# T5-bias attention followed by a mixture of adapters: PV by head, logits merged into the adapter product, gates on GpSimd, x transposed by DMA

## The chip, the cores and the metric

One NeuronCore of a Trainium2 chip runs the kernel. The time is that of the whole launch on the device, in microseconds. The engines are TensorE (PE in the profile, with its weight loads as PEld), VectorE (DVE), ScalarE (ACT), GpSimd (POOL) and SyncE (SP), which only issues transfers. Each engine takes its own instructions strictly in order and waits on semaphores for the others.

## The reference

Two stages. Shapes: B = 8 batches, H = 8 heads, S = 576 positions, D = 64; the mixture sees N = 4608 rows of 512, with E = 8 experts of rank r = 16.

```
scores = q @ k.T / sqrt(D) + bias_table[bucket(|i-j|)]      # per batch and head
attn   = softmax(scores);   x = attn @ v                    # x: 4608 x 512
logits = x @ w_gate                                         # 4608 x 8
top two of the 8 experts; w = softmax over those two logits
out    = x + sum over the two experts e of w_e * (x @ A[e]) @ B[e]
```

## The kernel before, in words

**Units of work.** A *pair* is two heads of one batch; there are 32 pairs, four to a batch. Of the 576 positions 512 form four main tiles of 128, and the last 64, the *tail*, are handled for two heads at a time, so that they fill 128 partitions.

**One pair.** SyncE loads k, v and q in fp32 (`nat_dma`, `q_dma`; two 128 KB transfers each for k and v, one of 256 KB for q). GpSimd casts them to bf16 (`ck_`, `cq_`, `cv_`, all through `bcopy`, L140). TensorE transposes k and q (`T_pe`, L249) and VectorE copies the result out of PSUM (`T_ev`, L255). Five score chunks follow (`qk`, L266 for the four main ones). ScalarE takes the exponential of each 128x1024 chunk (`softmax_exp`, L286). VectorE multiplies the band near the diagonal by a table of bias factors (`band`, L295); both of its inputs are in SBUF. Then `pv` multiplies by v in six parts, for both heads inside each part (L310, L317, L325), into one PSUM tile of two banks. `norm1` takes the reciprocal of the row sums (L330) and `norm2` writes the normalised x in bf16 (L338), both for the two heads together. The first part of the next pair's `pv` waits for `norm2`, since there is one such PSUM tile.

**One mixture**, once for each of the first seven batches, after its fourth pair: TensorE transposes x (`mx_pe`, L349, and `mxt_pe`, L361, for the tail) and VectorE copies the results (`mx_ev`, L355, `mxt_ev`, L366). `lp_pe` (L379) computes the logits as products 8 columns wide. `gate_chain` (L388 to L436) turns them into gates: nine small steps, all but the exponential on VectorE. `z_pe` (L443) multiplies x by A, 128 columns wide. `z_ev` (L452) multiplies that by the gates while it reads PSUM. `zT_pe` and `zT_ev` transpose once more, `o_pe` (L468) multiplies by B, `o_ev` (L473) adds x, and `o_st` (L477) stores two tiles of 512 KB through SyncE. The tails of two batches are done together, in odd batches. The last batch has its own code (`final`), which the change leaves nearly as it is.

**Tails of k, q and v** are loaded by SyncE once per batch (`tail_dma`, `vtail_dma`: six transfers of 64 KB).

**What sets the order.** The text of the kernel does not run in the order in which it is written. Each step is entered with `add(engine, cost, function, deps, due)`; a planner at the end (L984 to L1013) walks all engines in modelled time, picks for each the ready step with the earliest due time, and so writes out a fixed order for every engine. The costs and due times are constants in the code. Buffer counts also shape it: five load buffers (`loads`), three for cast k and q (`nat`), two PSUM banks for everything small (`misc_ps`, the ring `ms`), two score tiles, two banks for `pv`, three x tiles, three output tiles.

Of the kernel before, what the change touches and what calls it, by code (L numbers as in the profile page):

```python
# [27 lines left out]
def kernel(  # L28
# [28 lines left out]
    DVE, PL, AC, SY, PE = nc.vector, nc.gpsimd, nc.scalar, nc.sync, nc.tensor  # L57
# [14 lines left out]
    class Op:  # L72
        __slots__ = ("eng", "cost", "lat", "fn", "deps", "due", "ring", "end", "done",
                     "users", "left", "ready", "n", "dma", "ps")

    QA = 0
    WARM = 40
    LAT = {"PE": 190, "ACT": 190, "DVE": 110, "PL": 200, "SP": 5000}
# [3 lines left out]
    def add(eng, cost, fn, deps=(), due=0.0, lat=None, ring=None, nb=0.0, dma=None, ps=False):  # L82
        o = Op()
        o.ps = ps
        o.dma = dma
        o.eng, o.cost, o.fn, o.due, o.ring = eng, cost, fn, due, ring
        o.lat = LAT[eng] if lat is None else lat
        o.deps = [d for d in deps if d is not None]
        o.end, o.users, o.done, o.ready, o.n = None, [], False, nb, len(ops)
        ops.append(o)  # L90
        return o
# [37 lines left out]
    Ab = cp.tile([128, 4, ER], BF16, tag="Ab")  # L129
    Wb = cp.tile([128, 4, E], BF16, tag="Wb")  # L130
# [12 lines left out]
    CC = {"PL": 650, "DVE": 330, "ACT": 520}  # L143
# [20 lines left out]
    def vtail_dma(b, e):  # L164
        if e == 0:
            stg[(b, "vtf")] = ldp.tile([128, HP, D], FP32, name="vtf", tag="vtf", bufs=2)
        SY.dma_start(out=stg[(b, "vtf")][e * 64:(e + 1) * 64],
                     in_=v[b, :, S4:, :].rearrange("(c e) p d -> e p c d", e=2)[e])

    def load(i):  # L170
        t0 = 5.0 * i
        nk = (0, 3000, 8500, 11000, 13000)[i] if i < 5 else 6500 + 1030 * (t0 - 12)
        nv = (4000, 9500, 12000, 15000)[i] if i < 4 else 6500 + 1030 * (t0 - 8)
# [9 lines left out]
    def loadt(b, due):  # L183
        n = 0.0 if b == 0 else 14000.0 if b == 1 else 6500 + 1030 * due
        for w in range(2):
            for e in range(2):
                en = "SP"
                R["lt", b, w, e] = add(en, 550, lambda w=w, e=e, en=en: tail_dma(b, w, e, en), [g_("ct", b - 2)],
                                       due + .01 * e, nb=n, dma=290)
        for e in range(2):  # L190
            R["lvt", b, e] = add("SP", 550, lambda e=e: vtail_dma(b, e), [g_("cvt", b - 2)],
# [106 lines left out]
    def pv(i, part):  # L298
        b, hp = divmod(i, HP)
        vn, vt = vnb[i], vts[b % 2]  # L300
        if part == 0:
            a = acp.tile([128, 2, S4], FP32, name="pv", tag="pv")
            st[(i, "acc")] = a[:, :, 0:5 * D1].rearrange("p h (s d) -> p h s d", s=5)
        acc = st[(i, "acc")]
        if part < 4:
            p = probs.pop((i, part))
            for h in range(2):
                for s in range(4):
                    o = h * 512 + s * 128
                    PE.matmul(acc[:, h, s, :], lhsT=p[:, o:o + 128], rhs=vn[:, part, h, :],  # L310
                              start=(part == 0 and s == 0), stop=False,
                              skip_group_check=True)
        elif part == 4:
            p = probs[(i, 4)]
            for g in range(4):
                for h in range(2):
                    PE.matmul(acc[:, h, 4, :], lhsT=p[:, g * 128:(g + 1) * 128],  # L317
                              rhs=vn[:, g, h, :], start=False, stop=False,
                              skip_group_check=True)
        else:  # L320
            p = probs.pop((i, 4))
            for s in range(5):
                l = p[:, 512 + s * 128:640 + s * 128] if s < 4 else ptt[b][:, hp, :]
                for h in range(2):
                    PE.matmul(acc[:, h, s, :], lhsT=l, rhs=vt[:, hp, h * D1:(h + 1) * D1],  # L325
                              start=False, stop=True, skip_group_check=True)

    def norm1(i):
        rc = sp.tile([128, 2, 5], FP32, name="rc", tag="rc")
        DVE.reciprocal(rc, st[(i, "acc")][:, :, :, D])  # L330
        st[(i, "rc")] = rc

    def norm2(i, s0=0, s1=5):
        b, hp = divmod(i, HP)
        acc, rc = st[(i, "acc")], st[(i, "rc")]
        if hp == 0:
            xs[b] = xp.tile([128, 5, H, D], BF16, name="x", tag="x", bufs=3)
        DVE.tensor_tensor(  # L338
            xs[b][:, s0:s1, 2 * hp:2 * hp + 2, :].rearrange("p s h d -> p h s d"),
            acc[:, :, s0:s1, :D],  # L340
            rc[:, :, s0:s1].unsqueeze(3).to_broadcast((128, 2, s1 - s0, D)), op=ALU.mult)


    def mx_pe(b, half, t2):
        if t2 == 0:
            st[(b, "xps", half)] = msp.tile([128, 4, 256], BF16, name="xps", tag="ms")
        ps = st[(b, "xps", half)]
        for c in range(4):
            PE.transpose(ps[:, c, t2 * 128:(t2 + 1) * 128],  # L349
                         xs[b][:, 2 * half + t2, 2 * c:2 * c + 2, :], ident)  # L350

    def mx_ev(b, half):
        if half == 0:
            st[(b, "m")] = xp.tile([128, 4, S4], BF16, name="xT", tag="xT")
        DVE.tensor_copy(st[(b, "m")][:, :, half * 256:(half + 1) * 256],  # L355
                        st.pop((b, "xps", half)))

    def mxt_pe(b):
        st[(b, "xtps")] = ps = msp.tile([128, 4, 2, 64], BF16, name="xtps", tag="ms")
        for c in range(4):  # L360
            PE.transpose(ps[:, c].rearrange("p f q -> p (f q)"),  # L361
                         xs[b][:, 4, 2 * c:2 * c + 2, :], ident)

    def mxt_ev(b, hf):
        s = slice(hf * 64, (hf + 1) * 64)
        DVE.tensor_copy(xts[(b // 2) % 2][s, :, b % 2, :], st[(b, "xtps")][s, :, hf, :])  # L366
# [5 lines left out]

    def lp_pe(b, w, nt, t0, t1):
        if t0 == 0:
            st[(b, w, "lp")] = msp.tile([128, nt, E], FP32, name="lp", tag="ms")
        lp, xT = st[(b, w, "lp")], xT_of(b, w)
        for t in range(t0, t1):
            for c in range(4):
                PE.matmul(lp[:, t, :], lhsT=xT[:, c, t * 128:(t + 1) * 128],  # L379
                          rhs=Wb[:, c, :], start=(t == 0 and c == 0), stop=(c == 3),  # L380
                          skip_group_check=True)
# [6 lines left out]
    def gate_chain(b, w, nt, pre, due):  # L388
        key = (b, w)
        S_ = lambda n: st[key + (n,)]  # L390

        def lg():
            src = S_("lp") if w != "L" else st["zl"][:, 512:552].rearrange("p (t e) -> p t e", e=E)
            DVE.tensor_copy(sm_(b, w, nt, "lg", [128, nt, E]), src)

        def mx(t):
            if t == 0:
                sm_(b, w, nt, "m8", [128, nt, 8])
            DVE.max(out=S_("m8")[:, t, :], in_=S_("lg")[:, t, :])

        def df():
            DVE.tensor_tensor(sm_(b, w, nt, "df", [128, nt, E]), S_("lg"),
                              S_("m8")[:, :, 0:1].to_broadcast((128, nt, E)),
                              op=ALU.subtract)

        def mk():
            DVE.tensor_tensor(sm_(b, w, nt, "mk", [128, nt, E]), S_("lg"),
                              S_("m8")[:, :, 1:2].to_broadcast((128, nt, E)), op=ALU.is_ge)

        def ex():  # L410
            AC.activation(sm_(b, w, nt, "ex", [128, nt, E]), S_("df"), ACT.Exp)

        def me():
            DVE.tensor_tensor(S_("mk"), S_("mk"), S_("ex"), op=ALU.mult)

        def sm():
            DVE.tensor_reduce(sm_(b, w, nt, "sm", [128, nt]), S_("mk"), axis=AX.X, op=ALU.add)
# [4 lines left out]
        def gt_():  # L422
            DVE.tensor_tensor(sm_(b, w, nt, "gate", [128, nt, E], BF16), S_("mk"),
                              S_("sm").unsqueeze(2).to_broadcast((128, nt, E)), op=ALU.mult)

        d = dv(nt * 8, False)
        a = add("DVE", d, lg, pre, due)
        R["lg", b, w] = a
        ms = [add("DVE", 70, lambda t=t: mx(t), [a], due + .01) for t in range(nt)]
        f = add("DVE", d, df, ms, due + .02)  # L430
        m = add("DVE", d, mk, ms, due + .04)
        x = add("ACT", 110, ex, [f], due + .03)
        e = add("DVE", d, me, [m, x], due + .05)
        s = add("DVE", d, sm, [e], due + .06)
        s = add("DVE", 70, rs, [s], due + .07)
        return add("DVE", d, gt_, [s], due + .08)  # L436

    def z_pe(b, w, t0, t, key):
        if t == t0:
            st[(b, w, "zp", t0)] = msp.tile([128, 2, ER], FP32, name="zp", tag="ms")  # L440
        xT = xT_of(b, w)
        for c in range(4):
            PE.matmul(st[(b, w, "zp", t0)][:, t - t0, :],  # L443
                      lhsT=xT[:, c, t * 128:(t + 1) * 128], rhs=Ab[:, c, :],
                      start=(t == t0 and c == 0), stop=(c == 3), skip_group_check=True)

    def z_ev(b, w, nt, t0, t1):
        n = t1 - t0
        if t0 == 0:
            sm_(b, w, nt, "zt", [128, nt, ER], BF16)  # L450
        zp = st.pop((b, w, "zp", t0))
        DVE.tensor_tensor(  # L452
            st[(b, w, "zt")][:, t0:t1].rearrange("p t (e r) -> p (t e) r", e=E),
            zp[:, 0:n].rearrange("p t (e r) -> p (t e) r", e=E),
            st[(b, w, "gate")][:, t0:t1].rearrange("p t e -> p (t e)").unsqueeze(2)
            .to_broadcast((128, n * E, r)), op=ALU.mult)
# [19 lines left out]
    def o_st(b, t):  # L476
        SY.dma_start(out=out[b * S:b * S + S4, :].rearrange("(p j) c -> p j c", j=4)[:, t - 1:t + 1],  # L477
# [96 lines left out]
    def weights():  # L574
# [9 lines left out]
        R["Ab"] = add("PL", 650, lambda: PL.tensor_copy(  # L584
            Ab, A_f.rearrange("p c e r -> p c (e r)")), ls, 15)
        R["Wb"] = add("PL", 100, lambda: PL.tensor_copy(Wb, W_f), [w_], 15)
# [39 lines left out]
    def mixture(b):  # L626
        due = 20.0 * (b + 1) + 4.5
        odd = b % 2 == 1
        nrm = [R["n2", 4 * b + hp] for hp in range(HP)]
# [5 lines left out]
        xe = []  # L635
        for half in range(2):
            d = D_(1.0)
            a0 = add("PE", 4 * mm(128), lambda h=half: mx_pe(b, h, 0), nrm + [g_("z", b - 2)], d,
                     ring=("ms",))
            a1 = add("PE", 4 * mm(128), lambda h=half: mx_pe(b, h, 1), [a0], d)  # L640
# [411 lines left out]
```

## Time and profile before

| | |
|---|---|
| times of two runs | 223.85 and 227.63 us, median 225.74 us |
| the profiled execution | 226.69 us, of which the span is 224.9 us |
| TensorE clock granted over the profiled execution | 0.947 |
| PE, DVE, ACT, POOL busy | 195.3, 185.1, 166.5, 89.5 us |
| data moved | 39.90 MB, mean 177 GB/s |

The page divides the span into 40 equal slices, and prints for each engine its busy share in tenths. Groups of instructions are listed as: source line, engine, operation, output and inputs, count, then total busy time and the mean of one, then the idle time just before them and what ended it. Consecutive instructions of one engine overlap a little in the record, so a mean can be longer than the step from one to the next. In the tail of the program, from about 209 us on, only the last batch's mixture is left.

### The profile page before, as it was taken

To read this page: it belongs to the slowest core of one execution; us is meant where nothing else is said; L and a number is where in the kernel's file an instruction comes from. 1 tells how busy PE (TensorE), PEld (TensorE's weight loads), DVE (VectorE), ACT (ScalarE), POOL (GpSimd) and SP (SyncE) were. 2 spreads that over 40 slices of the span, in tenths; PEclk is the share of its full clock that TensorE was granted. 3 is DMA by queue.
4 is the path that set the end of the run, shared out by engine and by line. 5 is a ranking of instruction groups with operands and counts; after the bars stand their busy time and mean duration, and the time that the engine had idled before them with its cause. 6 is when DMAs were issued, how large, how long until landed. Compare 5 with 4: busy or idle time off the path is not lost.

```text
span 224.9 us, 7541 instructions
## 1 busy us (share of the span) xinstructions
PE 195.3 (87%) x3019; PEld 137.3 (61%) x3019; DVE 185.1 (82%) x475; ACT 166.5 (74%) x189; POOL 89.5 (40%) x159
## 2 busy tenths in 40 slices
PE   7729995999989989999999799999999899998750
PEld 7425663667656665677676566776677666776410
DVE  4437784789899999999989989998989899989461
ACT  4516895798888889889986699898968799784111
POOL 6764635565654463544461534444253121000000
PEclk9975898599999999999999999999999999999887
DMA  5799889699798978987797789889970023102224
GB/s 137 169 231 179 208 129 240 163 227 229 175 234 279 210 201 214 274 237 174 185 321 168 169 214 270 245 206 243 319 175 3 0 96 119 29 0 97 93 102 131
DMA packets 99706, 39.90 MB, mean 177 GB/s; under 512 B 87648, under 2 KB 96640, under 8 KB 99672
## 3 DMA queue, kind: packets, MB, share of 16 engines
q1 hardware_dynamic: 98960, 38.76, 67.5%
q8 instruction: 23, 0.38, 0.7%
q0 software_dynamic: 160, 0.39, 0.6%
q10 hardware_dynamic: 552, 0.28, 0.4%
q14 instruction: 11, 0.09, 0.1%
HBM read 29.97 MB, written 9.45 MB: 175 GB/s over the span
## 4 chain that ended last, share of the span: by engine, by line
DVE 46%; PE 36%; DMA 7%; issue 4%; ACT 2%; SPq 2%; POOL 1%; POOLq 0%; DVEq 0%; ACTq 0%
DVE p L295 13%; PE pv L310 9%; DVE x L338 8%; PE sc L266 8%; DVE o L473 5%; PE kqps L249 4%; DVE kqT L255 4%; DMA MHr<-g_d 3%; DVE xT L355 3%; DVE rc L330 2%; PE xps L349 2%; PE pv L317 2%; ACT p L286 2%; DMA kf<-in_k_dram 2%; PE pv L325 2%
## 5 line engine op out<-in xcount | busy, mean ns | idle before, releaser
L286 ACT ACTIVATE p<-sc 128x1024 bf16<-128x1024 f32 x160 | 156.6, 1022 | 35.6 <-PE sc L266 17.6
L295 DVE TENSOR_TENSOR p<-p,M 128x512 bf16<-128x512 bf16 (+1 forms) x128 | 68.4, 547 | 2.4 <-ACT p L286 1.6
L310 PE MATMUL pv<-vn,p 128*128 128x65 bf16 x1024 | 53.0, 196 | 10.9 <-DVE p L295 5.5
L310 PEld LDWEIGHTS <-p 128*128 128x128 bf16 x1024 | 41.7, 99 | 28.7 <-issue 9.1
L266 PE MATMUL sc<-kqT 64*128 64x512 bf16 x256 | 51.3, 398 | 0.4
L140 POOL CAST kb<-kf 128x512 bf16<-128x512 f32 x31 | 19.9, 641 | 47.5 <-PE kqps L249 20.7
L140 POOL CAST vn<-vf 128x512 bf16<-128x512 f32 x32 | 21.3, 665 | 26.1 <-PE pv L317 11.3
L338 DVE TENSOR_TENSOR x<-pv,rc 128x640 bf16<-128x640 f32 (+2 forms) x33 | 26.4, 802 | 0.9
L140 POOL CAST qb<-qf 128x512 bf16<-128x512 f32 x31 | 22.2, 715 | 9.9 <-DMA qf<-in_q_dram 5.4
L255 DVE COPY kqT<-kqps 128x1024 bf16<-128x1024 bf16 x31 | 21.2, 683 | 5.8 <-PE kqps L249 5.5
L266 PEld LDWEIGHTS <-kqT 64*128 64x128 bf16 x256 | 12.7, 93 | 12.8 <-issue 4.1
L473 DVE TENSOR_TENSOR o<-dl,x 128x512 f32<-128x512 f32 x28 | 18.5, 675 | 1.0 <-PE dl L468 1.0
L249 PE MATMUL kqps<-ident,kb 128*128 128x128 bf16 x128 | 13.1, 227 | 2.7 <-POOL kb L140 1.8
L140 POOL CAST tl<-tf 64x512 bf16<-64x512 f32 x16 | 10.8, 672 | 10.0 <-DMA tf<-in_q_dram 9.6
L317 PE MATMUL pv<-vn,p 128*128 128x65 bf16 x256 | 13.9, 197 | 0.0
L325 PE MATMUL pv<-vt,p 128*128 128x65 bf16 x256 | 13.6, 197 | 0.0
L317 PEld LDWEIGHTS <-p 128*128 128x128 bf16 x256 | 11.3, 100 | 3.3 <-issue 2.0
L249 PE MATMUL kqps<-ident,qb 128*128 128x128 bf16 x128 | 13.1, 227 | 0.1
L325 PEld LDWEIGHTS <-p 128*128 128x128 bf16 x256 | 11.3, 100 | 2.2 <-issue 0.5
L271 PE MATMUL sc<-tlT,kqT 128*128 128x128 bf16 x128 | 12.6, 221 | 0.0
L277 PE MATMUL sc<-kqT,tlT 128*128 128x512 bf16 x32 | 12.4, 387 | 0.0
L249 PEld LDWEIGHTS <-kb 128*128 128x128 bf16 x128 | 8.5, 101 | 5.5 <-issue 2.6
(126 smaller groups left out, 271.9 us busy)
## 6 DMA issues: line engine op xcount, KB each, us to landing
kf<-in_k_dram SPq DMA_DIRECT2D x64, 128.0 KB, 3.3
vf<-in_v_dram SPq DMA_DIRECT2D x64, 128.0 KB, 3.6
qf<-in_q_dram SPq DMA_DIRECT2D x31, 256.0 KB, 3.5
out_dram<-o SPq DMA_DIRECT2D x14, 512.0 KB, 3.9
tf<-in_k_dram SPq DMA_DIRECT2D x16, 64.0 KB, 3.5
tf<-in_q_dram SPq DMA_DIRECT2D x16, 64.0 KB, 3.0
vtf<-in_v_dram SPq DMA_DIRECT2D x16, 64.0 KB, 3.2
out_dram<-ol SPq DMA_DIRECT2D x4, 256.0 KB, 2.5
```

The lines of the kernel that those rows point to most:

```text
L140: e.tensor_copy(o, i)
L249: PE.transpose(ps[:, w, j * 128:(j + 1) * 128], t[:, j], ident)
L255: DVE.tensor_copy(kqT[i], st[(i, "kqps")])
L266: PE.matmul(sc[:, h * 512:(h + 1) * 512], lhsT=t[s, 0, c * 128:(c + 1) * 128], rhs=t[s, 1, :], start=True, stop=True)
L271: PE.matmul(sc[:, g * 128:(g + 1) * 128], lhsT=t[:, 0, g * 128:(g + 1) * 128], rhs=tt[:, 1, hp, :], start=(g == 0), stop=True, skip_group_ ...
L286: AC.activation(p, st.pop((i, c, "sc")), ACT.Exp, scale=scale)
L295: DVE.tensor_tensor(pm, pm, M[:, 2 * hp:2 * hp + 2, :, x0:x0 + q1 - q0], op=ALU.mult)
L310: PE.matmul(acc[:, h, s, :], lhsT=p[:, o:o + 128], rhs=vn[:, part, h, :], start=(part == 0 and s == 0), stop=False, skip_group_check=True)
L317: PE.matmul(acc[:, h, 4, :], lhsT=p[:, g * 128:(g + 1) * 128], rhs=vn[:, g, h, :], start=False, stop=False, skip_group_check=True)
L325: PE.matmul(acc[:, h, s, :], lhsT=l, rhs=vt[:, hp, h * D1:(h + 1) * D1], start=False, stop=True, skip_group_check=True)
L338: DVE.tensor_tensor(xs[b][:, s0:s1, 2 * hp:2 * hp + 2, :].rearrange("p s h d -> p h s d"), acc[:, :, s0:s1, :D], rc[:, :, s0:s1].unsqueeze ...
L473: DVE.tensor_tensor(st[(b, t // 2, "o")][:, t % 2], st.pop((b, t, "dl")), xs[b][:, t].rearrange("p h d -> p (h d)"), op=ALU.add)
```

## The change

- `pv`, `norm1` and `norm2` work for one head at a time, each head with a PSUM bank of its own (`pv0`, `pv1`); the number of products is the same.
- `mx_pe`, `mx_ev`, `mxt_pe` are gone. SyncE issues five DMA transposes per mixture (`mx_dma`), from x in SBUF to xT in SBUF; two GpSimd copies (`mxt_ev`) place the tail.
- `lp_pe` is gone. w_gate is appended to A (`AW`, 136 columns), so `z_pe` yields logits and x @ A in one product. `z_ev` only copies the result to SBUF (`zf`); the gates are applied afterwards on GpSimd (`z_gate`).
- In `gate_chain` four of the steps (`df`, `sm`, `me`, `gt_`) move to GpSimd for all mixtures but the last; the copy `lg` is gone there.
- The tail loads from the second batch on, and the output stores of `o_st`, are issued by GpSimd in place of SyncE.
- The planner may hold a GpSimd cast of k, q or v (from the tenth pair on) back by up to 1.5 us and place it where VectorE is about to start a step that reads PSUM; such a cast then gets a real wait on the VectorE instruction before that step. In the order that results, 40 of the 94 casts carry a wait on VectorE. Loads get earlier due times.

```diff
-    Ab = cp.tile([128, 4, ER], BF16, tag="Ab")
-    Wb = cp.tile([128, 4, E], BF16, tag="Wb")
+    AW = cp.tile([128, 4, ER + E], BF16, tag="AW")
+    Ab, Wb = AW[:, :, 0:ER], AW[:, :, ER:]
...
-                en = "SP"
+                en = "PL" if b else "SP"
...
-    def pv(i, part):
+    def pv(i, part, h):
...
-            a = acp.tile([128, 2, S4], FP32, name="pv", tag="pv")
+            a = acp.tile([128, S4], FP32, name=f"pv{h}", tag=f"pv{h}")
...
-        DVE.reciprocal(rc, st[(i, "acc")][:, :, :, D])
+        DVE.reciprocal(rc, st[(i, h, "acc")][:, :, D])
...
+        DVE.tensor_tensor(xs[b][:, s0:s1, 2 * hp + h, :], acc[:, s0:s1, :D],
+                          rc[:, s0:s1].unsqueeze(2).to_broadcast((128, s1 - s0, D)), op=ALU.mult)
...
+    def mx_dma(b, t):
+        if t == 0:
             st[(b, "m")] = xp.tile([128, 4, S4], BF16, name="xT", tag="xT")
-        DVE.tensor_copy(st[(b, "m")][:, :, half * 256:(half + 1) * 256],
-                        st.pop((b, "xps", half)))
...
+        if t < 4:
+            o = st[(b, "m")][:, :, t * 128:(t + 1) * 128]
+        else:
+            o = st[(b, "xq")] = xp.tile([128, 4, 128], BF16, name="xq", tag="xq")
+        SY.dma_start_transpose(out=o, in_=xs[b][:, t].rearrange("p h d -> p (h d)"))
...
+        ge_, G = ("DVE", DVE) if w == "L" else ("PL", PL)
...
+            G.tensor_tensor(sm_(b, w, nt, "df", [128, nt, E + 2]), LG(0, E + 2),
+                            LG(E, E + 1).to_broadcast((128, nt, E + 2)), op=ALU.subtract)
...
     def z_ev(b, w, nt, t0, t1):
...
+        DVE.tensor_copy(st[(b, w, "zf")][:, t0:t1, 0:ER + E],
+                        st.pop((b, w, "zp", t0))[:, 0:t1 - t0])
+
+    def z_gate(b, w, nt, t0, t1):
...
+        PL.tensor_tensor(
+            st[(b, w, "zt")][:, t0:t1].rearrange("p t (e r) -> p t e r", e=E),
+            st[(b, w, "zf")][:, t0:t1, 0:ER].rearrange("p t (e r) -> p t e r", e=E),
+            st[(b, w, "gate")][:, t0:t1].unsqueeze(3).to_broadcast((128, n, E, r)), op=ALU.mult)
...
-        SY.dma_start(out=out[b * S:b * S + S4, :].rearrange("(p j) c -> p j c", j=4)[:, t - 1:t + 1],
+        PL.dma_start(out=out[b * S:b * S + S4, :].rearrange("(p j) c -> p j c", j=4)[:, t - 1:t + 1],
...
+        if o.eng == "DVE":
+            if o.ps and lastv is not None and free["PL"] <= t + 120:
+                ws = [c for c in cand["PL"] if c.win and start_of(c) <= t + 120]
+                if ws:
+                    c = min(ws, key=lambda x: (x.due, x.n))
+                    c.after = lastv
+                    place(t + 60, c)
+            lastv = o
```

## The prediction

> **What bounds the kernel now.** I read the page's slices first, to find stages, then the busy time of the engines in the steady stretch, then groups, waits, and SyncE's own timeline.
>
> ```profile
> PE   7729995999989989999999799999999899998750
> DVE  4437784789899999999989989998989899989461
> ACT  4516895798888889889986699898968799784111
> POOL 6764635565654463544461534444253121000000
> DMA  5799889699798978987797789889970023102224
> ```
>
> Three stages: a start of some 46 us, a steady stretch with PE and DVE both at 9 in nearly every slice, and from 209 us a tail. The DMA row stays at 7 to 9 until slice 30 and then drops to nothing: all loads are in by 168 us. The steady stretch, from the gates of one mixture (50.87) to those six mixtures later (194.69), with busy time by engine (PE, PEld, DVE, ACT, POOL), clock, DMA share and GB/s:
>
> ```profile
> 50.87:194.69 143.82, 136.17 (x2235) 96.60 (x2233) 134.59 (x341) 122.74 (x138) 60.13 (x93) 1.00 0.74 195
> ```
>
> 143.82 / 6 = 23.97 us per batch. Of that PE is busy 22.70 (94.7%), DVE 22.43 (93.6%), ACT 20.46, POOL 10.0. So TensorE and VectorE bound together; relief for one alone gives nothing. The groups that the change touches:
>
> ```profile
> L295 DVE TENSOR_TENSOR p<-p,M 128x768 bf16<-128x768 bf16 x64 | 40.0, 633 | 0.9 <-ACT p L286 0.5
> L295 DVE TENSOR_TENSOR p<-p,M 128x512 bf16<-128x512 bf16 x64 | 29.5, 461 | 1.5 <-ACT p L286 1.1
> L338 DVE TENSOR_TENSOR x<-pv,rc 128x640 bf16<-128x640 f32 x31 | 25.5, 822 | 0.9
> L140 POOL CAST qb<-qf 128x512 bf16<-128x512 f32 x31 | 22.2, 715 | 9.9 <-DMA qf<-in_q_dram 5.4 <-PE kqps L249 1.9 <-PE sc L279 0.7
> L355 DVE COPY xT<-xps 128x1024 bf16<-128x1024 bf16 x14 | 9.6, 685 | 1.3 <-PE xps L349 1.3
> L551 POOL DMA_DIRECT2D MHr<-g_d x2 | 1.3, 646 | 0.0
> ```
>
> The last row is the price of a transfer issued from GpSimd. From the waits: PE stands 10.9 us in all before the first `pv` part for `norm2` (6.8 at its weight loads, 4.1 at the products). SyncE's timeline at 117 us:
>
> ```profile
> 117.90 1.99 SPq L155 DMA_DIRECT2D qf<-in_q_dram  x1
> 119.94 0.61 SPq L161 DMA_DIRECT2D tf<-in_k_dram  x1
> 120.61 0.60 SPq L161 DMA_DIRECT2D tf<-in_q_dram  x1
> 121.26 0.61 SPq L161 DMA_DIRECT2D tf<-in_k_dram  x1
> 121.92 0.61 SPq L161 DMA_DIRECT2D tf<-in_q_dram  x1
> ```
>
> SyncE issues without a pause, and a q load that takes 0.5 us elsewhere takes 2.0 here: I read this as the transfers pushing back. Loads are no slack resource until 168 us.
>
> **What the Trainium skill says.** *SBUF — State Buffer*, "Who interferes with whom": a VectorE instruction with two SBUF inputs and a GpSimd instruction that reads SBUF exclude each other for a whole instruction, while a PSUM reader does not collide. The trace agrees: the 128x512 band takes 0.41 us with GpSimd quiet, up to 1.0 beside a cast, and casts range from 0.61 to 0.94. *VectorE: DVE Perf Modes*, "The three transpose paths" gives 1309 ns for a 128x128 DMA transpose; *DMA: Bandwidth & Descriptors*, "Latency and other measured facts" gives 261 GB/s for DMA transposes. No run here shows one yet, and for 128x512 bf16 (128 KB) these are 5.2 us (four in series) and 0.5 us: ten times apart. *GPSIMD Engine Reference*, "Elementwise — side-by-side cycle accounting", has 4497 ns for a two-input step of 2048 fp32, an estimated 0.56 us for 256.
>
> **The change part by part**, per batch with a mixture.
>
> *TensorE.* Gone: 20 transposes at 60 ns (four follow in 0.24 us in the timeline) = 1.20, and 16 logit products, plus 4 every second batch, at 43 ns (eight in 0.34) = 0.77. The 8 added columns are 3% of 128, under 0.1 on 0.9 us. PV by head keeps count and shape. Net -1.9: 22.70 becomes 20.8.
>
> *VectorE.* Busy time in the steady stretch over six batches: L355 8.21, L366 3.42, L394 1.47, L402 1.60, L414 3.96, L417 1.39, L423 2.15, in all 22.2, or 3.7 per batch, gone. Added by splitting the norm: L338 is 424 for 256 elements and 822 for 640, so 490 for 320; twice that less 822 is 0.16. The reciprocal is 168 for 4 and 215 for 10 elements; twice 175 less 215 is 0.13. Four pairs: +1.2. The plain copy of 272 replaces a multiplication of 256 at 416, about even. Net -2.5. Freed bands: 51.98 us over 98 is 530 each, against 480 uncontended (0.41 and 0.55 by form), 16 x 0.05 = 0.8 at most; with 40 of 94 casts tied I take 0.3. DVE: 22.43 becomes 19.6. If no cast is kept clear, 19.9, and PE still hides that.
>
> *GpSimd.* Now 10.0. Added: eight transfers at 0.65 = 5.2; two z products at 0.7 = 1.4, plus 0.2 for odd tails; four small steps at 0.23 (copies of that size took 0.18 to 0.23) = 0.9, plus 0.4; two xT copies at 0.4 = 0.8. Sum 8.9: 18.9 per batch. It fits in 22, with an eighth to spare, and is no longer an engine whose lateness is free.
>
> *SyncE.* Gone: six tail issues at 0.61 and two stores at 0.36 = 4.4. Added: five transposes. A k load is 0.5 to 0.6 to issue; I bound a transpose by that below and by the 5.2 us above. Up to 0.9 SyncE breaks even. The transposes wait for the fourth pair's norms, and the next k, q and v loads stand behind them in SyncE's order; there the transposes stand after k loads five to eight pairs ahead, about as far as five load buffers and three cast buffers allow anyway, so I cost that wait at nothing.
>
> *DMA engines.* Busy work until 168 us: 20 x 0.85 + 26 x 0.82 + 122 x 0.88 = 145.7 us. Against that come 30 transposes (six mixtures) before the last k load. I take 0.65 us each: a k load is also 128 KB, and counting every transfer in k loads by its bytes and pieces gives about 220 of them in 145.7 us. Lower end 0.5, upper 5.2. The last pair's k must land 32 us before the end (its transposes are at 193.6 of 224.9), two before the stream ends. So the end is at least (145.7 + 30 x 0.65) / 0.88 + 30 = 218, or 210 if the share reaches 0.92.
>
> *New waits.* The gates now hop VectorE, GpSimd, ScalarE, GpSimd, VectorE, GpSimd, TensorE. Behind the waiting exponential on ScalarE stand the score exponentials; behind a tied cast, the store and gate steps of GpSimd; behind a late zT, all of TensorE. One such hop already costs (ScalarE for `df`: 1.9 us over four waits in 50 to 190 us). ScalarE's spare, 22 - 20.5, covers about one. I charge 0.6 us per batch, bounds 0 and 2. PV by head gives back up to half of the 10.9 us, since head 0 of the next pair can start after half a norm; I leave it as the reserve for PE's idle share.
>
> *Sum.* If PE keeps its present idle time of 1.27 us, a batch takes 22.0, 1.95 less; seven mixtures give 13.7. Less 7 x 0.6 = 4.2 of new waits: -9.5. The profiled execution's 226.69 becomes 217.2, which the DMA bound of 210 to 218 also allows. The median is 0.95 below that execution; I predict 217.
>
> **The rivals.**
> 1. *GpSimd paces.* Its 18.9 plus in-order waits for VectorE, transposes and stores comes to about 23.5. For it: every engine takes a result from it, and 5.2 us of issue is new. Against: casts run several us ahead. Result: the old period, 222 to 229.
> 2. *The transposes starve the loads* (the other side). Place: SyncE's queue and the 16 engines until the last load. With 1.3 us each: (145.7 + 39) / 0.88 + 30 = 240. It turns against the change from 0.92 us per transpose, where the bound passes 226.7, and to slower by 2% from 1.05. For it: DMA share 0.88 already, and the wide prices. Against: the nearest row.
> 3. *Nothing new waits*, bands run free, PV by head fills PE's gaps: 226.7 - 13.7 - 4 = 209, if the DMA share rises to 0.92.
> 4. *The ties do nothing*: bands stay at 530 ns. 0.3 us per batch on DVE, under PE: no visible change from 217.
>
> **How the numbers follow.** My forecast with 3 and 4: 0.56. Rival 1: 0.20, nearly all within 2%, which is about what the two runs before (1.7% apart) let one tell. Rival 2: 0.20, and 0.04 for a GpSimd that is far over its budget: slower. The range from 209 to 236 leaves out the far end of rival 2.
>
> **What would show it.** Right: PE and DVE busy per batch near 20.8 and 19.6, a period near 22.5, transposes landing like k loads, few PE waits for a cast. Wrong: POOL at 9 in every slice; PE or ScalarE waiting for GpSimd by more than 1 us per batch; casts waiting on k or q loads late in the run, or the DMA row still busy after 190 us.

## The result, and the profile after

The changed kernel takes 265.16 us (263.64 to 266.68, two runs) against 225.74 us: a ratio of 1.180, interval 1.160 to 1.201. Ratios, here and below, and the times of the experiments count fast runs alone (a run over 1.5% above the fastest of its kernel is a slow one), so a ratio is not quite the quotient of two medians. I had predicted 217, with 236 as the upper end. The profiled execution took 266.68 us. The top of its page, the rows of the engines and of DMA in 40 slices:

```profile
span 264.8 us, 7157 instructions
...
PE 200.7 (76%) x2755; PEld 134.1 (51%) x2755; DVE 174.3 (66%) x461; ACT 166.1 (63%) x189; POOL 147.0 (55%) x286
...
PE   7457975796996679944976967888889978887850
DVE  4367868357986567745572784477867788896761
ACT  4527977497895537951594735399819975986020
POOL 5887677528860965826394595245556275434100
DMA  5699899989995998992964739574978732730405
```

No engine is at 9 throughout any more. Where before PE and DVE stood at 9 together, all rows now dip and recover together, and the DMA row, which dropped to nothing at slice 31, is at 7 or more in slices 31, 32 and 35. The steady stretch, from the gates of the first mixture to those of the seventh (columns as in the stretch shown of before):

```profile
63.90:239.20 175.30, 140.03 (x1939) 93.21 (x1941) 121.82 (x320) 117.11 (x131) 99.97 (x189) 0.90 0.75 171
```

That is 175.30 / 6 = 29.2 us per batch instead of 24.0, with PE busy 23.3, DVE 20.3, ACT 19.5 and POOL 16.7. (The stretch holds 95 of the band products and that of before 98, so these counts are some 3% low.) I had predicted 20.8 for PE, 19.6 for DVE and 18.9 for POOL. VectorE and GpSimd do about the work that I had counted. TensorE is busy 2.5 us longer. The clock granted to it is 0.90 here and was 1.00 before; no run separates how much of the 2.5 us that is, or whether it costs time, but TensorE is idle for 5.9 of the 29.2 us. What is new is that every engine waits. Each line gives the total of a wait in us, how often it came, and the longest. Before:

```profile
ACT p L286 <- PE sc L266: 17.6, 27, 2.3
DVE rc L330 <- PE pv L325: 4.1, 5, 1.1
POOL kb L140 <- PE kqps L249: 20.7, 8, 4.8
SPq L149 <- POOL kb L140: 1.4, 2, 1.1
```

After, and below that SyncE's own:

```profile
ACT p L300 <- PE sc L280: 56.5, 26, 9.1
POOL xTt L65 <- DMA xq<-x: 25.4, 6, 6.2
DVE rc L65 <- PE pv L332: 18.0, 14, 4.1
```

```profile
SPq L163 <- POOL kb L65: 17.7, 7, 5.6
SPq L356 <- DVE x L65: 11.3, 2, 10.6
SPq L163 <- POOL vn L65: 8.6, 6, 3.2
```

ScalarE waits 56.5 us for scores (17.6 before), GpSimd 25.4 us for a transpose, SyncE 26.3 us for casts of k and v that have to free a load buffer (1.4 for k before). Gone is GpSimd's wait for TensorE to free a buffer of cast k, 20.7 us before: the casts no longer run as far ahead as their buffers allow. Of the 11.3 us that SyncE stands for norms, 10.6 come after the last load has left, at 214.79 us, and hold no load up. One mixture shows how these hang together (timeline from 105 us; the bracket is idle time just before and what ended it):

```profile
105.64 6.26 SPq L356 DMA_TRANSPOSE xT<-x  x4
...
111.95 1.28 SPq L356 DMA_TRANSPOSE xq<-x  x1
...
115.83 0.41 PE L432 MATMUL zp<-AW,xT 128*128 128x136 bf16 x4 [2.36 <-DMA xT<-x]
...
117.23 0.40 POOL L65 COPY xTt<-xq 64x256 bf16<-64x256 bf16 x1 [2.95 <-DMA xq<-x]
...
120.81 1.19 POOL L65 TENSOR_TENSOR zt<-zf,gate 128x256 bf16<-128x256 f32 x2
121.48 0.28 PE L454 MATMUL ztps<-ident,zt 128*128 128x128 bf16 x2 [3.13 <-POOL zt L65]
121.94 0.61 POOL L65 CAST kb<-kf 128x512 bf16<-128x512 f32 x1
...
128.96 2.85 ACT L300 ACTIVATE p<-sc 128x1024 bf16<-128x1024 f32 x3 [9.10 <-PE sc L280]
```

SyncE needs 7.6 us just to issue five transposes (105.64 to 113.23), and sends no load in that time. The last one is in at 117.23, 11.6 us after the first was issued. The kernel before, in one mixture of its run:

```profile
115.82 0.82 DVE L338 TENSOR_TENSOR x<-pv,rc 128x640 bf16<-128x640 f32 x1
...
119.83 0.68 DVE L355 COPY xT<-xps 128x1024 bf16<-128x1024 bf16 x1
```

There the second of the two xT copies is done at 120.51, 3.9 us after the norm. In the changed kernel, on GpSimd, the next pair's cast of k stands behind six transfers (108.23 to 111.93), two casts of tails, the xTt copies, four gate steps and two z products. It runs at 121.94 and is done at 122.55. TensorE takes it up at 125.73, behind the products with B, which have waited for the same late gates. The first products for its scores start at 128.43, and ScalarE has stood for 9.10 us.

### The profile page after: what moved, and what is told of

It is laid out like the page before. It is cut to its first block, busy times and chain, and to the rows that moved or that the text cites. A ratio compares the mean times of both kernels' runs of the same rounds, so it can differ in the third digit from the quotient of the medians.

```text
span 264.8 us, 7157 instructions
## 1 busy us (share of the span) xinstructions
PE 200.7 (76%) x2755; PEld 134.1 (51%) x2755; DVE 174.3 (66%) x461; ACT 166.1 (63%) x189; POOL 147.0 (55%) x286
## 4 chain that ended last, share of the span: by engine, by line
PE 27%; DVE 22%; DMA 13%; SPq 12%; POOL 10%; issue 10%; ACT 4%; POOLq 0%; DVEq 0%; ACTq 0%
PE pv L323 8%; PE sc L280 6%; DVE p L65 6%; DVE x L65 5%; SPq L163 4%; DMA qf<-in_q_dram 4%; ACT p L300 3%; SPq L356 3%; DMA kf<-in_k_dram 3%; DVE o L65 3%; DMA xT<-x 2%; PE kqps L263 2%; DVE kqT L65 2%; POOL tf L65 2%; DVE zf L65 2%
## 5 line engine op out<-in xcount | busy, mean ns | idle before, releaser
L300 ACT ACTIVATE p<-sc 128x1024 bf16<-128x1024 f32 x160 | 156.2, 1025 | 73.5 <-PE sc L280 56.5
L65 DVE TENSOR_TENSOR p<-p,M 128x512 bf16<-128x512 bf16 (+1 forms) x128 | 70.4, 560 | 19.3 <-ACT p L300 19.0
L323 PE MATMUL pv<-vn,p 128*128 128x65 bf16 x1024 | 57.0, 204 | 14.0 <-DVE p L65 6.9
L323 PEld LDWEIGHTS <-p 128*128 128x128 bf16 x1024 | 45.4, 104 | 33.7 <-issue 13.9
L65 POOL CAST vn<-vf 128x512 bf16<-128x512 f32 x32 | 20.4, 637 | 29.2 <-DVE p L65 11.0
L65 DVE COPY kqT<-kqps 128x1024 bf16<-128x1024 bf16 (+1 forms) x33 | 22.0, 670 | 13.2 <-PE kqps L263 13.0
L65 DVE TENSOR_TENSOR x<-pv,rc 128x320 bf16<-128x320 f32 (+1 forms) x65 | 30.0, 476 | 0.6
L65 POOL CAST qb<-qf 128x512 bf16<-128x512 f32 x31 | 20.6, 665 | 11.3 <-PE dl L461 2.7
L65 DVE RECIPROCAL rc<-pv 128x5 f32<-128x5 f32 x64 | 11.0, 186 | 18.0 <-PE pv L332 18.0
L65 POOL COPY xTt<-xq 64x256 bf16<-64x256 bf16 x14 | 6.1, 433 | 29.6 <-DMA xq<-x 25.4
L332 PE MATMUL pv<-vt,p 128*128 128x65 bf16 x256 | 15.9, 197 | 0.0
L461 PE MATMUL dl<-Bb,zT 128*128 128x512 bf16 x28 | 12.2, 477 | 4.4 <-DVE zT L65 2.3
L327 PE MATMUL pv<-vn,p 128*128 128x65 bf16 x256 | 15.2, 198 | 0.0
L432 PE MATMUL zp<-AW,xT 128*128 128x136 bf16 x112 | 10.8, 227 | 5.0 <-DMA xT<-x 4.9
```

Of the source, the lines that this page charges most:

```text
L65: self.inst = f(*a, **k)
L300: AC.activation(p, st.pop((i, c, "sc")), ACT.Exp, scale=scale)
L323: PE.matmul(acc[:, s, :], lhsT=p[:, o:o + 128], rhs=vn[:, part, h, :], start=(part == 0 and s == 0), stop=False, skip_group_check=True)
L327: PE.matmul(acc[:, 4, :], lhsT=p[:, g * 128:(g + 1) * 128], rhs=vn[:, g, h, :], start=False, stop=False, skip_group_check=True)
L332: PE.matmul(acc[:, s, :], lhsT=l, rhs=vt[:, hp, h * D1:(h + 1) * D1], start=False, stop=True, skip_group_check=True)
L432: PE.matmul(st[(b, w, "zp", t0)][:, t - t0, :], lhsT=xT[:, c, t * 128:(t + 1) * 128], rhs=AW[:, c, :], start=(t == t0 and c == 0), stop=(c ...
```

## The experiments

The order of every engine is planned anew for each variant, so a difference of a few us between two of them may come from the order alone; no run shows how much. Each ratio is against runs of the kernel before on the same chip, whose medians lie between 224.0 and 226.6. Four theories were in play at first: the tie waits (A), the order written by holding casts back (B), the late transposes (C), GpSimd's transfers (D). Every kernel computes the whole reference; those with unread transposes issue five transfers a batch more than that needs.

**The waits of the ties removed, order kept.**

```diff
-        if o.after is not None:
+        if False:
```

> The changed kernel in the same written order on every engine; only the 40 added waits of casts on VectorE are left out. Theory A (the waits themselves stall GpSimd): back to 240 us or less. Theory B (the order that the holding back of casts writes is what costs): 258 to 265, about as the changed kernel. Theory C (the DMA transposes are late and everything queued behind them waits): 258 to 265 as well.

Measured: 271.96 us, ratio 1.210 (1.199 to 1.222). It became slower by 7 us. The waits themselves are not the cause. They even do what they are for. The band products of this run:

```profile
L65 DVE TENSOR_TENSOR p<-p,M 128x768 bf16<-128x768 bf16 x64 | 43.5, 683 | 1.9 <-ACT p L300 1.7
L65 DVE TENSOR_TENSOR p<-p,M 128x512 bf16<-128x512 bf16 x64 | 32.4, 506 | 18.3 <-ACT p L300 18.0
```

That is 75.9 us; with the waits, in the same order, it is 71.5 (the lines of the changed kernel stand further below). What else their absence costs is open (in that trace GpSimd waits 40.9 us for the transposes in place of 25.4).

**No cast held back or tied.**

```diff
-        if i > 8:
+        if i > 99:
             for n_ in ("ck", "cq", "cv"):
                 R[n_, i].win = True
```

> The changed kernel with no cast held back by the planner (no patience of 1.5 us, no ties), all else as changed. Theory B: most of the loss is gone, 215 to 228 us. Theory C: stays above 245, because the transposes, the copies that wait for them and the transfers on GpSimd are as before. Theory A alone: same as the run without the tie waits.

Measured: 240.28 us, ratio 1.071 (1.063 to 1.079). 25 of the 39 us are gone, which lies between the two cases. GpSimd's wait for the transposes stays, at 19.0 us.

**x transposed on TensorE and VectorE, as before; the rest as changed.**

```diff
-        SY.dma_start_transpose(out=o, in_=xs[b][:, t].rearrange("p h d -> p (h d)"))
+            PE.transpose(ps[:, c, t2 * 128:(t2 + 1) * 128],
+                         xs[b][:, 2 * half + t2, 2 * c:2 * c + 2, :], ident)
...
+        DVE.tensor_copy(st[(b, "m")][:, :, half * 256:(half + 1) * 256],
+                        st.pop((b, "xps", half)))
```

> The changed kernel with x transposed on TensorE and copied by VectorE as in the kernel before; casts still held back, transfers and gates still on GpSimd. Theory C: back to 225 to 232 us. Theory B: 245 to 262, since the casts are still held back.

Measured: 238.64 us, ratio 1.062 (1.052 to 1.072). 26.5 of the 39 us are gone, with the casts still held back; this too lies between the cases.

**Tail loads and output stores issued by SyncE.**

```diff
-                en = "PL" if b else "SP"
+                en = "SP"
...
-        PL.dma_start(out=out[b * S:b * S + S4, :]
+        SY.dma_start(out=out[b * S:b * S + S4, :]
```

> The changed kernel with tail loads and stores issued by SyncE as before. Theory D (5.2 us of transfer issue per batch on GpSimd delay its casts): 235 to 245 us. Theories B and C: 250 to 265; a little may come back from the shorter GpSimd queue, a little be lost on SyncE.

Measured: 255.51 us, ratio 1.137 (1.128 to 1.147): 10 us gone. A falls, and D as the main cause; B and C each look like two thirds of the loss, which can't both be added.

**B and C undone together, then the transfers, then the gates as well.** The first is the two edits above in one kernel. The second adds the edit of the transfers. The third adds `ge_, G = "DVE", DVE` and the z product on VectorE, which leaves PV by head, the merged logits and the earlier loads (the expectation calls them later).

> Both at once: x is transposed on TensorE and VectorE as in the kernel before, and no cast is held back or tied. Each alone took some 25 us off the 265. Theory X (the two losses lie on top of each other: the late transposes and the late casts are two ends of the same loop, SyncE waiting for GpSimd and GpSimd for SyncE, so breaking it once is most of it): 230 to 238 us. Theory Y (two separate losses that add): 265 - 25 - 26 = 214 us. If GpSimd's added work (transfers, gate steps, z products) is a third loss of its own, the time stays over 226 us in either case.

> As the run with both, and the tail loads and the output stores are issued by SyncE again, 8 transfers a batch of 0.6 us less on GpSimd. If their issue on GpSimd is what still costs: 5 to 10 us under the run with both. If GpSimd's time is covered once nothing waits in a loop (my step that GpSimd has room): within 2 us of it.

> What is left of the change: PV by head, the logits merged into the z product, the later loads. The gate steps and the products of gate and z are on VectorE again, x is transposed on TensorE, the transfers are SyncE's, no cast is held back. By my prediction's own steps TensorE gives 1.2 us a batch and VectorE 0.3 plus what the merged logits save, so 218 to 223 us. If PV by head and the merged logits gain nothing by themselves: 226. If they are what loses (a rival that I have not tested so far): over 230 us.

Measured: 232.34 (ratio 1.023, 1.017 to 1.029), 231.69 (1.022, 1.014 to 1.030) and 230.38 us (1.015, 1.010 to 1.020). Taking both out gives back 33 us and not 51. Put the other way round: held-back casts without DMA transposes cost 6.3 us (238.64 against 232.34), DMA transposes without held-back casts 7.9 (240.28 against 232.34), and the two together 32.8. Each makes the other more costly. With both gone, GpSimd's transfers cost nothing that shows and its gate steps under 2 us. GpSimd is still busy 143.3 us in the first of these three, against 147.0 in the changed kernel: its load is not what costs.

**Unread transposes.** TensorE's transposes feed the mixture, and SyncE issues the five DMA transposes of each batch beside them, into tiles of their own.

```diff
+    def mx_dma(b, t):
+        o = xp.tile([128, 4, 128], BF16, name=f"sh{t}", tag=f"sh{t}", bufs=2)
+        SY.dma_start_transpose(out=o, in_=xs[b][:, t].rearrange("p h d -> p (h d)"))
```

Three runs: beside casts that are not held back, beside casts that are, and beside held-back casts with a constant tile as the source, so that the transposes wait for no norm.

> As the run with both, TensorE's transposes feeding the mixture, but SyncE also issues the five DMA transposes of each batch, into tiles that nobody reads. It keeps their issue time, their wait on SyncE ahead of the loads, and their work on the DMA engines, and leaves out only that the mixture waits for them. If the loss by the DMA transposes is that z and GpSimd wait for their landing: within 2 us of the run with both. If it is their traffic and SyncE's queue: it rises to about the 240 us that the change without holding back took.

> As the run with TensorE's transposes in the changed kernel (casts held back, 238.7 us), and SyncE also issues the five DMA transposes of each batch into tiles that nobody reads. If the 26 us of the transposes there are the mixture's wait for a late landing: 237 to 243 us (the unread ones cost 4 us without holding back). If they are SyncE's queue, with the loads behind the transposes, and the traffic: 255 to 265 us.

> As the run with unread transposes beside held-back casts (253.7 us), but the unread transposes read a constant tile (slices of M) and so wait for no norm; five a batch on SyncE, of the same size, booked at about the same times. If the 15 us are SyncE's wait for the norms with the loads behind it: 238 to 243 us, as without them. If they are the issue time on SyncE (6.3 us a batch) and the traffic on the DMA engines: 249 to 257 us.

Measured: 236.43 us (ratio 1.040, 1.034 to 1.046), 251.31 us (1.109, 1.103 to 1.116) and 245.54 us (1.087, 1.080 to 1.094). Each falls between its two cases, so the cost has parts. Where casts are held back it runs from 238.6 to 245.5 with the constant source (6.9 us: issue on SyncE and traffic), to 251.3 with x as the source (5.8: SyncE standing at the transposes for the norms, with loads behind), to 265.2 when the mixture also reads them (13.9: the late landing, with the xTt copies in GpSimd's queue). These labels are my reading: the constant transposes also leave at other times (the second five from 58.88 us, those of x from 76.01), and the last step also takes the transposes off TensorE and the copies off VectorE. Where casts are not held back the same 8 us is 4.1 by their presence and 3.9 by the reading (232.3, 236.4, 240.3).

The traffic can be read from the queues (packets, MB, share of 16 engines' span; q1 is SyncE's, q0 GpSimd's). With TensorE's transposes and held-back casts:

```profile
q1 hardware_dynamic: 85520, 28.67, 56.3%
q0 software_dynamic: 3520, 10.49, 14.2%
```

The same with unread transposes of x (span 249.6):

```profile
q1 hardware_dynamic: 104560, 33.26, 66.1%
q0 software_dynamic: 3520, 10.49, 14.1%
```

And with those of a constant (span 243.6), with its DMA row:

```profile
DMA  5799989999999999999999989989969534000415
...
q1 hardware_dynamic: 104560, 33.26, 71.3%
q0 software_dynamic: 3520, 10.49, 15.7%
```

70.5% of 236.1 us is 166.5 us of all 16 engines; 80.2% of 249.6 is 200.2; 87.0% of 243.6 is 211.9. For 35 transposes that is 33.7 and 45.4 us, 0.96 and 1.30 us each; the pair without holding back gives 1.19. The higher figures are from fuller engines; I take it that packet times there include waiting for one another. With the constant source the DMA row stands at 8 or 9 from slice 3 to slice 29, and I read that run as paced by its transfers.

**The xTt copies on VectorE.**

```diff
-        PL.tensor_copy(xts[(b // 2) % 2][s, :, b % 2, :], st[(b, "xq")][s, :, s])
+        DVE.tensor_copy(xts[(b // 2) % 2][s, :, b % 2, :], st[(b, "xq")][s, :, s])
```

> The changed kernel with one step moved: the two small copies of the transposed fifth slice (xTt from xq) are on VectorE again, as in the kernel before. In the changed kernel they wait 25.4 us in all at the head of GpSimd's queue for a transpose to land, with the casts behind them. If this queueing behind a late transpose is what the transposes cost: most of the 26 us that the run with TensorE's transposes got back, 238 to 245 us. If the wait only moves on (to VectorE, where the band products are queued behind it, or to the gate steps): 255 to 265 us.

Measured: 267.43 us, and up to 273.71 in single runs. These runs spread, so I read only that none came under the changed kernel. Taking the copies off GpSimd's queue does not help; the first case falls, and the second was too low.

**The gates and z products on VectorE, the rest as changed.**

> The changed kernel with its gate steps and the products of gate and z on VectorE. If these are what holding back lets in ahead of the casts on GpSimd, the casts come early again: about the 240 us of the run without holding back. If GpSimd's transfers and xTt copies are enough for that: over 255 us.

Measured: 256.05 us, ratio 1.128 (1.122 to 1.134): 9 us gone, as with the transfers. Each kind of added GpSimd step costs some 10 us where casts are held back and transposes go by DMA, and under 2 where both are gone; no run took only one of the two away.

**Holding back alone**, beside PV by head and merged logits and then in the kernel before:

> As the run with PV by head and the merged logits alone (230.4 us), and the casts are held back and tied as in the changed kernel; GpSimd has nothing but casts there. Only the written order of GpSimd's work differs in kind. If holding back hurts through the other GpSimd work that is let in ahead of the casts: within 2 us of 230. If it hurts by itself, through casts that come late: over 234 us. If the ties do what they are for, VectorE's band products (617 ns in the changed kernel and 610 without ties) come under 550 ns and the time goes under 228.

> The kernel before with its casts held back and tied to VectorE's PSUM reads, nothing else. If holding back is worth the 3.1 us that it gave in the run with PV by head and merged logits: 222 to 224.5 us, which would beat both kernels. If it is worth nothing in the kernel before: 225 to 228 us. My prediction took 0.3 us of VectorE's time a batch for it, 2 us in all.

Measured: 227.14 us (1.008, 1.004 to 1.012), 3.2 us under the same kernel without it (1.6 by the two ratios); and 225.36 us against 226.59 (0.994, 0.991 to 0.997). Where GpSimd has nothing but casts, holding back costs nothing. The 0.6% by which the second lies under the kernel before is less than the 2% from which I call two kernels different, and it does not come from freed bands: the band products of that run take 38.5 + 32.1 = 70.6 us, and 69.5 before. What gives the 0.6% is open.

**What is left: loads, PV by head, merged logits.**

```diff
-        nk = (0, 3000, 8500, 11000, 13000)[i] if i < 5 else max(14000, 6500 + 1030 * (t0 - 20))
+        nk = (0, 3000, 8500, 11000, 13000)[i] if i < 5 else 6500 + 1030 * (t0 - 12)
```

> As the run with PV by head and the merged logits alone, with the earliest times at which the planner books the k, q and v loads as in the kernel before. In that run's trace TensorE stood 2.9 us for tail casts whose loads were issued behind others. If the booked load times are what makes it slower than the kernel before: 225 to 227 us. If they are of no account: within 1.5 us of 230.4.

> As the run with the loads as before, and PV is one group for both heads again, with one reciprocal and one normalization. Only the merged logits (and the sum of the two exponentials in place of a masked sum) are left of the change. PV by head costs VectorE 64 x (180 + 480) - 32 x (215 + 822) ns = 9.1 us of work in these traces. If the last 4 us of the loss are that: 222 to 226 us, at or under the kernel before. If PV by head pays for itself on TensorE: at or over the run with the loads as before.

> The kernel before with PV by head alone: two accumulators, so that one head's normalization lies beside the other head's products, for 9.1 us more of VectorE's work. In the kernel before TensorE waited 10.9 us (6.8 and 4.1) for that normalization. If the split pays: 220 to 224 us. If VectorE's added work takes it back: 225 to 229 us. If it takes more than that: 230 to 234 us.

> The kernel before with PV by head and with its casts held back and tied, the two parts that looked useful (2.3 us in the comparison of the runs with merged logits, and 3.1 us for holding back). If they add on top of the kernel before: 219 to 223 us, under both kernels. If their gain was only a repair of the merged logits' cost: 225 to 229 us.

Measured: 229.75 us with the loads as before (1.019, 1.009 to 1.029), so they don't matter. 232.06 with the merged logits alone (1.025, 1.015 to 1.034); there VectorE also does the products of gate and z that the change gives to GpSimd. 229.07 with PV by head alone (1.011, 1.007 to 1.016). 227.08 with PV by head and holding back (1.010, 1.005 to 1.015). Neither part gains. That the two together (229.75) cost less than the merged logits alone may be the order. The waits for the normalization in the kernel before with PV by head (6.8 and 4.1 before):

```profile
PEld L309 <- DVE x L331: 9.8, 21, 1.1
PE pv L309 <- DVE x L331: 6.4, 14, 1.0
PE pv L309 <- DVE rc L323: 1.4, 3, 0.7
```

17.6 us instead of 10.9, and VectorE is busy 189.4 us against 185.1. In the run with merged logits alone these waits are 23.0 us and VectorE's busy time 192.0. So there are two readings, and no run separates them: two half-sized norms each stand in VectorE's full queue and lengthen the hand-over, or VectorE simply has 4.3 and 6.9 us more to do. TensorE's busy time can't decide it: 33 of the 3019 products are missing from the record of the run with PV by head.

## Why the prediction was wrong

The term that failed by most is "New waits: 0.6 us per batch, bounds 0 and 2". The period rose by 5.2 us where my sum had it fall by 1.95.

**The counts of work** on VectorE and GpSimd were near, as shown above; TensorE's came out 2.5 us higher, at a lower clock. The sum failed in what it did with them: it turned 1.95 us less of TensorE's work into 1.95 us less of period. In the kernel before two engines are both over 93% busy and hand work to each other. PV by head and the merged logits, which I put at a gain, give none when run alone (1.1 and 2.5% over the kernel before). I read that as a longer hand-over; that VectorE had more to do is the rival above. (Three slips, none of weight: 217.2 less 0.95 is 216.3, 8 columns are 6% of 128, and casts range up to 1.05 us, not 0.94.)

**"I cost that wait at nothing"** (SyncE at the norms, loads behind): this failed, by some 6 us in the runs with held-back casts (245.5 and 251.3). The lead of the loads that I counted on was there: 39 k transfers, those of 19 to 20 pairs, have left when the third mixture's transposes start at 105.64 us. The lead of the casts was not. A load can't be issued until a cast has freed its buffer, and those are the 26 us of SyncE's waits above. They come with holding back, but their length does not measure the loss: with held-back casts and TensorE's transposes SyncE waits 19.0 us for casts of k, 17.4 for q and 11.8 for v, and that run is 26.5 us faster.

**"DMA engines. I take 0.65 us each"** was mis-sized: 0.96 to 1.30 measured, past the 0.92 from which I had let rival 2 turn the result. It also lies above my lower end of 0.5, which I had worked out from a page's rate; here the measurement decides. I had also not costed that transfers moved to GpSimd take more of the engines' time: 166.1 us in all with them there and 156.9 with the same bytes issued by SyncE, in the two runs with neither holding back nor DMA transposes. The Trainium skill (*DMA: Bandwidth & Descriptors*, "Issuing engines are not separate DMA queues") says that transfers from all issuers interleave on the same 16 engines; the runs agree, and a change of queue was no relief. With 0.96 and these 9.2 us my own bound is (145.7 + 28.8 + 9.2) / 0.88 + 30 = 239, beside 240.3 for the kernel without holding back. That agreement is luck: with the 1.19 measured without holding back the bound is 247, above what was measured, and in that kernel the DMA share that I had divided by as 0.88 is 1.07 from 20 to 180 us. So the packet times of different transfers overlap, and they are no fixed work for a bound. What the runs show for rival 2 is the 7.9 us that DMA transposes cost without holding back. On *SyncE*, the issue took 1.26 us, between my bounds of 0.5 to 0.6 and 5.2, where I had break-even at 0.9. The planner of the changed kernel books 1280 ns of SyncE for each transpose, so this price stood in its code; the 520 ns of DMA that it books are about half of what was measured.

**New waits.** I had listed them one hop at a time, and only "behind a tied cast, the store and gate steps of GpSimd". It is the other way round: the casts stand behind the transfers, the gate steps and the xTt copies, since the planner lets every GpSimd step that is ready within 1.5 us go ahead of a held cast. I had costed holding back by its 40 ties alone. Its order costs 25 us beside the other GpSimd work and DMA transposes, 6.3 beside that work with TensorE's transposes (238.64 and 232.34), and nothing where GpSimd has casts only. That holding and late transposes multiply through the circle of load buffers (SyncE waits for casts, GpSimd for transposes, transposes for SyncE) is how I read the timeline; the runs show the sizes, not the circle itself.

**Rival 1** named the right engine and the wrong mechanism. POOL is at 55%, and my argument against it ("casts run several us ahead") was what broke. **Rival 4** was right in the number and not in the reason: bands take 39.3 + 32.2 = 71.5 us in the changed kernel and 69.5 before, so none were freed. But without the ties' waits they take 75.9 in the same order. The ties win back 4.4 of the 6.4 us that the rest of the change puts on the bands.

```profile
L65 DVE TENSOR_TENSOR p<-p,M 128x768 bf16<-128x768 bf16 x64 | 39.3, 617 | 2.4 <-ACT p L300 2.4
L65 DVE TENSOR_TENSOR p<-p,M 128x512 bf16<-128x512 bf16 x64 | 32.2, 503 | 16.9 <-ACT p L300 16.6
```

The price of *VectorE*'s split norm held to within 6% (490 and 175 ns predicted, 481 and 186 measured), and a z product on *GpSimd* took 0.67 us where I had estimated 0.56 and charged 0.7. Of the signs I had named for being wrong, the busy DMA row after 190 us came (8 and 7 in slices 31 and 32), and so did waits for GpSimd of over 1 us per batch (TensorE's weight loads 5.4 us for zt, 5.2 for tl and 3.9 for qb, ScalarE 4.1 for df, over seven batches); POOL at 9 in every slice did not, nor did casts wait long for loads (2.0 us for k). One sign of being right came as well: the transposes land like k loads.

## What to carry to other kernels

An engine at half load is no free place to move steps to if something urgent runs through it in order: price the move by what the urgent steps then stand behind, for every kind of step moved. A wait that is free because producers run ahead stops being free once another part of the same change takes that lead away, so cost the parts together: here two parts that cost 6 and 8 us alone cost 33 together. And where two engines are both over 90% busy and feed each other, less work on one is worth little if it puts work or a hand-over on the other.

## What the runs showed of the hardware

- A DMA transpose of a 128x512 bf16 tile takes 1.26 us to issue on SyncE (the median in the changed kernel), against 0.5 to 0.6 for a plain load of the same 128 KB, and adds 0.96 to 1.30 us to the packet time of the 16 DMA engines. It lands 2.9 and 2.5 us (medians of xT and xq) after its issue in the changed kernel, where a k load takes 4.4, and 4.7 us after it in the run with the constant source. I had expected it to be like a load in all three; it is so in the landing.
- The same eight transfers a batch took 9.2 us more of DMA engine time in the whole run when issued from GpSimd. The time did not follow (232.34 and 231.69 us).
- The busy share of the 16 DMA engines, as the profile counts it, can pass 1: 1.07 from 20 to 180 us in the run without holding back, and 1.10 in that with the constant source.
- With 40 of GpSimd's casts tied to VectorE's reads of PSUM the band products take 71.5 us, and in the same order without the ties 75.9.
